# Narrow attention blocks finished four at a time, and a new order for all engines, in an attention and two-layer feed-forward kernel

## The chip, the cores and the metric

The kernel runs on one core of one Trainium2 chip. The metric is device time in microseconds (us), from the start of the program to its end; lower is better. Five kinds of instruction streams matter: TensorE (PE), VectorE (DVE), ScalarE (ACT), GpSimd (POOL), and SyncE (SP), whose single queue issues every DMA of this program.

## What is computed

The weights are float64, all else float32; q, k, v have 4 batches of 8 heads of 576 rows of 64. Attention keeps only the scores within tau of the row's maximum; its output, 2304 rows of 512, goes through two feed-forward layers with 2048 hidden units.

```python
scores = scale * np.matmul(q, k.transpose(0, 1, 3, 2))
thresh = np.max(scores, axis=-1, keepdims=True) - tau
scores = np.where(scores >= thresh, scores, -1000000000.0)
scores = scores - np.max(scores, axis=-1, keepdims=True)
attn = np.exp(scores)
attn = attn / (np.sum(attn, axis=-1, keepdims=True) + 1e-09)
return np.matmul(attn, v)
...
x = np.ascontiguousarray(attn_out.transpose(0, 2, 1, 3)).reshape(B * S, H * D)
h = x @ w_in
g = np.where(pos, h, np.where(neg, 0.0, (h + beta) ** 2 / (4.0 * beta)))
x = (g @ w_out).astype(np.float32)
...
h = x @ w_in
g = h - np.tanh(h)
return (g @ w_out).astype(np.float32)
```

## The kernel before

**Attention** works on blocks of 128 query rows of one head (`units`). A block goes through scores (`u_qk`, line 570, into one of three PSUM pairs `s0` to `s2`), row maximum (`u_max`, DVE), exponential and threshold (`u_exp`, ACT), masking with the row sum as a by-product (`u_mask`, line 603, DVE), a split of the weights into two float16 parts (`u_hi` on ACT, `u_lo` on POOL), and one DMA transposition (`u_tr`). There are five phases. Phase 0 is batch 0's 512 main rows of each head, phase 1 is batch 1; both are "narrow" (`NARROW = (0, 1)`). There the product with v is `u_dot` (line 658): 14 small matmuls of 64 columns into a bank of the two-bank ring `ph`, block by block, and `u_put` (line 677) brings the 128x64 result to SBUF (tile `xw`) while it multiplies by the reciprocal of the row sum. The reciprocal costs two one-column DVE instructions per block in `u_mask`. In the last head pair of phase 0 (`DIRECT = (3,)`) the weights are turned by TensorE instead of by DMA (`u_turn`, into `s2`), and `u_dot` is five float32 matmuls with the raw v (`vr`). Phases 2 to 4 are "wide" and use `pv` (line 743) in place of `u_dot` and `u_put`. `x_split` (line 771) turns a head pair's output with TensorE (`ph<-idt,xw`) and splits it into `xh` and `xl`.

**The feed-forward part** is 160 steps `j = (T, M, s)`: five token tiles T (512 columns, the last 256), two layers M, sixteen slices s of the hidden units. A step is `m_h` (12 matmuls into a `ph` bank), `m_act`, `m_dve`, `m_split`, and `m_out` (12 matmuls into `s1`, `s2`). During T = 0 the weights are loaded as 64-bit numbers (`w64`), decoded on ACT and DVE (`w_dec`, tiles `top` and `wr`), split (`w_split`) and stored to device memory (`w_store`, `wf`); later tiles load the stored parts (`w_get`).

**The order** is planned while the program is built. `agenda` (line 964) gives every operation a due time in steps: blocks of phase 0 lie before step 0, phase 1 is spread over the 32 steps of T = 0, phases 2 and 3 over T = 1 and T = 2. `PRE` (line 88) moves the due time of each kind of operation forward by so many steps, with one column for the time before step 0, one for T = 0, one for T = 1 to 3 and one for T = 4. `Program.issue` (line 261) then lays out all five streams: whichever engine is free first takes, of the operations whose inputs are there by the planner's own durations, the one that is due first. Those durations are written in `dve`, `act`, `sub`, `mm`, `dma`, and `Program.run`. What comes out is a fixed order per engine; on the chip each engine works through its list and waits where an input is late.

```python
    for i in range(NU):
        k = when(i)
        for fn, o in zip((u_qk, u_max, u_exp, u_mask, u_hi, u_lo, u_tr), UNIT):
            at(k + o, fn, i)
        if not units[i][0].wide:
            k = snap(k + lag(units[i][0]))
            at(k, u_dot, i)
            at(k, u_put, i)
```

Of the kernel before, what the change touches and what calls it, by code (L numbers as in the profile page):

```python
# [21 lines left out]
D = 64  # L22
# [63 lines left out]
    "A",  # L86
]
PRE = {
    "load_k": (7.27, -15.44, 8.94, 0.00),
    "load_q": (3.73, 6.44, 24.95, 0.00),  # L90
    "m_act": (0.00, -5.32, -0.24, -7.95),
    "m_dve": (0.00, 11.52, -21.89, -14.88),
    "m_evac": (0.00, -4.26, 4.07, -23.40),
    "m_h": (0.00, -1.15, -0.74, 2.14),
    "m_out": (0.00, -3.74, -0.36, 2.07),
    "m_split": (0.00, -1.26, 7.97, 1.61),
    "prep_k": (-15.59, 0.87, 7.96, 0.00),
    "prep_q": (21.35, 4.08, -22.11, 0.00),
    "pv": (0.00, 0.00, 2.86, 0.00),
    "u_dot": (-4.92, -3.40, 0.00, 0.00),  # L100
    "u_exp": (23.08, 16.66, 42.89, 0.00),
    "u_hi": (10.52, 34.89, 8.23, 0.00),
    "u_lo": (-15.45, 16.69, 11.25, 0.00),
    "u_mask": (1.51, -2.24, 3.82, 0.00),
    "u_max": (10.16, -1.25, -4.45, 0.00),
    "u_put": (19.81, -1.30, 0.00, 0.00),
    "u_qk": (-1.85, 25.10, 3.18, 0.00),
    "u_tr": (5.19, -3.00, 19.56, 0.00),
    "v_load": (1.71, -6.79, 1.05, 0.00),
    "v_max": (5.82, -0.49, -4.93, 0.00),  # L110
    "v_sc1": (-2.99, 15.36, 1.20, 0.00),
    "v_sc2": (-2.52, -2.20, 18.08, 0.00),
    "v_split": (9.81, -2.61, 10.15, 0.00),
    "w_dec": (3.79, -9.16, 0.00, 0.00),
    "w_get": (0.00, 21.91, 4.43, 25.50),
    "w_load": (-7.83, 28.33, 0.00, 0.00),
    "w_split": (5.66, -2.05, 0.00, 0.00),
    "w_store": (27.74, -13.05, 0.00, 0.00),
    "x_split": (17.49, 19.09, -2.78, 0.00),
    "x_tail": (0.00, 12.50, 0.00, 0.00),  # L120
}
G_LO = [
    "PPPVPPPV",
# [39 lines left out]
class Program:  # L163
# [65 lines left out]
    def run(self, o, t):  # L229

        e = o.eng
        if e == "SP":
            turn = o.dur > 1000
            begin = max(self.dma, t + (1000 if turn else 900))
            self.dma = begin + o.serve
            self.free[e] = max(t + o.dur, begin - (2000 if turn else 4500)) + 60
            return t, self.dma + 1250
        if e == "PE":
            load, f0, f1 = self.load, self.free[e], t - 250
            fill = 0  # L240
# [92 lines left out]
def attention_moe_moe2(ctx: ExitStack, tc: tile.TileContext, qd, kd, vd, tau, w1, w2, ident, out):  # L333
# [61 lines left out]
    def dve(name, **kw):  # L395
        src = kw.get("in_", kw.get("in0"))
        n = max(width(kw["out"]), width(src))
        ins = [kw[k] for k in ("in_", "in0", "in1") if k in kw]
        on_chip = not any(in_psum(a) for a in ins)
        fast = name in ("tensor_scalar", "tensor_copy") and on_chip and n > 8  # L400
        dur = 150
        if n > 8:
            dur = n / (1.92 if fast else 0.96) + 150 + 50 * ("accum_out" in kw)
            dur += 60 * (fast and any(isinstance(kw.get(k), AP) for k in ("scalar1", "scalar2")))
# [75 lines left out]
    for b, mains, tail in plan:  # L480
        for hp in range(H // 2):
            t = Obj()
            t.ph = len(touches) // 4
            t.direct = t.ph == 0 and hp in DIRECT
            t.b, t.hp, t.first, t.mains, t.tail = b, hp, len(units), mains, tail
            t.wide = t.ph not in NARROW
            t.aT = [None, None]
            t.cols = [slice(0, HALF), slice(HALF, S)] if mains and tail else [slice(0, 512) if mains else slice(512, S)]
            t.xf = t.xt = None
            touches.append(t)  # L490
            if tail:
# [166 lines left out]
    def u_dot(i):  # L658
        t, e, m = units[i]
        u = U[i]  # L660
        v = VQ[t.ph, t.hp // 2]
        u.p = ph_r()
        if t.direct:
            for c in range(5):
                n = 128 if c < 4 else 64
                mm(u.p[:, 0:D], u.et[0:n, 128 * c:128 * c + 128], v.raw[0:n, 2 * (t.hp % 2) + e, c], c == 0, c == 4)
            return
        for x in range(2) if e is None else (e,):
            h = 2 * (t.hp % 2) + x
            o = u.p[:, 64 * x:64 * x + 64] if e is None else u.p[:, 0:64]  # L670
            for c in range(5):
                mm(o, u.at[:, c], v.t[:, h, c, x, :], c == 0, False)
                mm(o, u.at[:, c], v.t[:, h, c, 1 - x, :], False, False)
            for c in range(4):
                mm(o, u.at[:, 5 + c], v.t[:, h, c, x, :], False, c == 3)

    def u_put(i):
        t, e, m = units[i]
        u = U.pop(i)
        if e is None:  # L680
            t.xt = xt_r()
        elif t.xf is None:
            t.xf = xf_r()
        for x in range(2) if e is None else (e,):
            o = t.xt[:, 64 * x:64 * x + 64] if e is None else t.xf[:, 128 * m + D * e:128 * m + D * e + D]
            src = u.p[:, 64 * x:64 * x + 64] if e is None else u.p[:, 0:64]
            if t.direct:
                dve("tensor_scalar", out=o, in0=src, scalar1=u.rs, scalar2=None, op0=ALU.mult)
            else:
                h = 2 * (t.hp % 2) + x  # L690
                dve("tensor_scalar", out=o, in0=src, scalar1=u.rs, scalar2=VQ[t.ph, t.hp // 2].inv[:, h:h + 1],
                    op0=ALU.mult, op1=ALU.mult)
# [412 lines left out]
```

## Time and profile before

| what | value |
|---|---|
| time, median of 3 runs | 1089.78 us (1081.36 to 1090.7) |
| span of the profiled execution, first to last instruction | 1082.6 us |
| PE busy | 1030.0 us (95%) |
| DVE busy | 629.2 us (58%) |
| ACT busy | 632.4 us (58%) |
| POOL busy | 504.0 us (47%) |
| DMA queue of the program | 271.83 MB, 86.5% of 16 engines' span |

The profile shows one execution. Of it the page gives the span, and no separate time for what lies around it; the span is 0.1% above the fastest of the three runs and 0.7% below their median. Busy shares are means over stages that differ much, so the rows below are read by stage. A matmul's record covers its passage through a pipeline, so a busy PE is not a PE at its peak. DMA share is the mean busy share of 16 engines and can be over 1, since an engine can have two transfers in hand. Nearly all instructions carry line 354, that of the recording helper; they are told apart by tile names.

### The profile page before, as it was taken

Reading aid. Unit: us, or ns where it says so; the run is one execution under the profiler, and the core shown is the slowest. Engines: PE = TensorE matmul, PEld = TensorE weight load, DVE = VectorE, ACT = ScalarE, POOL = GpSimd, SP = SyncE. Lnnn points to the kernel's source line nnn. Section 1 sums busy time; section 2 is a strip of 40 time slices with the busy share of each in tenths; the row PEclk is TensorE's granted clock in tenths of the full one; section 3 lists DMA queues with packets and bytes.
Section 4 is the critical chain, followed back from the end, with each engine's and each line's share of the span. In section 5 each row is a group of like instructions: output and inputs, shape, how many; then the busy total and the mean of one; then the engine's idle time right before and its main releaser. Section 6 shows DMA issues by size and latency. Waiting matters only on the chain.

```text
span 1082.6 us, 17257 instructions
## 1 busy us (share of the span) xinstructions
PE 1030.0 (95%) x5826; PEld 831.0 (77%) x5826; DVE 629.2 (58%) x1380; ACT 632.4 (58%) x1158; POOL 504.0 (47%) x510
## 2 busy tenths in 40 slices
PE   5789999999999999999999999999999999998997
PEld 3567777767777788778888888778877878888986
DVE  5987978898898766674347665742253331113432
ACT  5778777768776777676457777764353332222332
POOL 3654778768686555445345555444333212220000
PEclk8999999999999999999999999999999999999999
DMA  6999999999999998889679988897586655557997
GB/s 148 176 229 335 313 319 320 297 275 353 352 336 314 315 243 231 226 227 232 209 206 277 266 212 217 211 230 207 171 269 194 178 189 183 188 193 285 369 343 248
DMA packets 231384, 272.93 MB, mean 252 GB/s; under 512 B 170240, under 2 KB 170368, under 8 KB 231296
## 3 DMA queue, kind: packets, MB, share of 16 engines
q1 hardware_dynamic: 231296, 271.83, 86.5%
q8 instruction: 46, 0.75, 0.3%
q14 instruction: 42, 0.34, 0.1%
HBM read 193.40 MB, written 38.27 MB: 214 GB/s over the span
## 4 chain that ended last, share of the span: by engine, by line
PE 70%; DVE 12%; ACT 8%; DMA 5%; issue 4%; POOL 1%; SPq 0%; ACTq 0%; DVEq 0%; POOLq 0%
PE ph L354 35%; PE s L354 35%; DVE small L354 3%; DMA w<-in_w_dram 2%; ACT e L354 2%; DVE wr L354 2%; DVE e L354 2%; DMA vr<-in_vd_dram 2%; DVE g L354 1%; DVE xw L354 1%; ACT a L354 1%; DVE ph L354 1%; DMA wo<-wf0o 1%; ACT top L354 1%; DMA at<-w 1%
## 5 line engine op out<-in xcount | busy, mean ns | idle before, releaser
L354 PE MATMUL ph<-xh,wi 128*128 128x512 f32 x1024 | 271.1, 399 | 4.0 <-DVE g L354 3.7
L354 POOL TENSOR_TENSOR a<-e,a 128x512 f16<-128x512 f32 x236 | 180.9, 785 | 188.9 <-ACT a L354 172.4
L354 POOL TENSOR_TENSOR gl<-g,gh 128x512 fp32r<-128x512 f32 x114 | 152.3, 1336 | 199.1 <-ACT gh L354 179.4
L354 PEld LDWEIGHTS ph<-xh,wi 128*128 128x128 f32 x1024 | 188.0, 189 | 45.4 <-DVE g L354 6.2
L354 PE MATMUL s<-gh,wo 128*128 128x512 f32 (+1 forms) x640 | 157.4, 377 | 5.2 <-ACT gh L354 1.9
L354 PE MATMUL s<-wo,gh 128*128 128x512 f32 x576 | 155.1, 398 | 1.1 <-ACT w L354 0.7
L354 PE MATMUL ph<-xl,wi 128*128 128x512 f32 x512 | 144.8, 396 | 0.2 <-DVE xl L354 0.2
L354 DVE SCALAR_TENSOR_TENSOR e<-s,small,e 128x576 f32<-128x576 f32 x129 | 104.8, 813 | 67.1 <-ACT small L354 66.4
L354 DVE TENSOR_REDUCE small<-s 128x1 f32<-128x576 f32 x144 | 108.2, 752 | 47.7 <-PE s L354 46.8
L354 ACT ACTIVATE gh<-g 128x512 fp32r<-128x512 f32 (+1 forms) x152 | 88.2, 581 | 78.5 <-DVE g L354 76.2
L354 DVE TENSOR_TENSOR g<-ph,t 128x512 f32<-128x512 f32 (+1 forms) x80 | 50.8, 635 | 142.2 <-ACT t L354 138.9
L354 PEld LDWEIGHTS s<-gh,wo 128*128 128x128 f32 x640 | 112.0, 191 | 26.4 <-ACT gh L354 4.2
L354 PEld LDWEIGHTS s<-wo,gh 128*128 128x128 f32 x576 | 105.2, 188 | 22.9 <-ACT gh L354 1.1
L354 ACT ACTIVATE e<-s,small 128x576 f32<-128x576 f32 x129 | 94.9, 736 | 44.6 <-DVE small L354 41.7
L354 ACT ACTIVATE t<-ph 128x512 f32<-128x512 f32 (+1 forms) x80 | 44.1, 552 | 120.6 <-PE ph L354 120.4
L354 PEld LDWEIGHTS ph<-xl,wi 128*128 128x128 f32 x512 | 95.9, 188 | 23.2 <-DVE xl L354 1.2
L354 PE MATMUL s<-gl,wo 128*128 128x512 f32 (+1 forms) x320 | 89.4, 381 | 4.5 <-ACT xh L354 2.1
L354 DVE TENSOR_TENSOR ph<-ph,t 128x512 f32<-128x512 f32 (+1 forms) x80 | 51.4, 643 | 70.1 <-ACT t L354 69.2
L354 ACT ACTIVATE t<-ph,small 128x512 f32<-128x512 f32 (+1 forms) x80 | 51.4, 642 | 66.4 <-PE ph L354 66.2
L354 ACT ACTIVATE a<-e 128x576 f16<-128x576 f32 x118 | 80.1, 679 | 6.8 <-DVE e L354 4.8
L354 PE MATMUL s<-wo,gl 128*128 128x512 f32 x288 | 82.3, 393 | 1.0 <-ACT w L354 1.0
L354 PEld LDWEIGHTS s<-gl,wo 128*128 128x128 f32 x320 | 57.6, 190 | 15.8 <-ACT xh L354 3.4
(107 smaller groups left out, 1513.6 us busy)
## 6 DMA issues: line engine op xcount, KB each, us to landing
w<-in_w_dram SPq DMA_DIRECT2D x64, 512.0 KB, 6.0
wi<-wf0i SPq DMA_DIRECT2D x64, 512.0 KB, 4.1
wo<-wf0o SPq DMA_DIRECT2D x64, 512.0 KB, 4.3
wi<-wf1i SPq DMA_DIRECT2D x64, 512.0 KB, 3.8
wo<-wf1o SPq DMA_DIRECT2D x64, 512.0 KB, 3.7
kr<-in_kd_dram SPq DMA_DIRECT2D x32, 288.0 KB, 4.4
wf0i<-wi SPq DMA_DIRECT2D x16, 512.0 KB, 6.1
wf0o<-wo SPq DMA_DIRECT2D x16, 512.0 KB, 5.6
```

The costliest lines, as they stand in the source:

```text
L354: P.add(eng, dur, lambda: fn(**kw), outs, ins, serve, lock, load)
```

## The change

In the narrow phases the four blocks of a head become a group. `u_mask` writes the row sums of the four blocks side by side and makes no reciprocal; `g_rs` makes one pair of four-column instructions per head; `g_dot` does the matmuls of all four blocks into one `ph` bank, one after the other; `g_put` moves 128x4x64 results with one `tensor_tensor` and the reciprocals broadcast over 64 columns. All three are due when the head's fourth block would have been. The 64-row tail blocks keep the old form. Over the whole program DVE loses 64 reciprocals, 64 one-column `tensor_scalar` and 64 `xw<-ph` of 64 columns, and gains 16 of each in the four-fold form; PE, ACT, POOL and SP have the same instructions as before. The planner's numbers change as well: a plain DMA now counts as later and slower (345 in place of 415 bytes per ns), a transposition as 1200 in place of 1100, an issue on SP as longer; and all of `PRE` is replaced, of which two lines stand here.

```diff
@@ PRE
-    "m_split": (0.00, -1.26, 7.97, 1.61),
+    "g_rs": (78.75, 171.00, 0.00, 0.00),
+    "m_split": (0.00, -1.81, 25.05, -140.59),
...
-            begin = max(self.dma, t + (1000 if turn else 900))
+            begin = max(self.dma, t + (1050 if turn else 1250))
...
-        rec("SP", 590 if n < 200e3 else 345, nc.sync.dma_start, serve=max(n / 415.0, 130) + 150 * (n < 400e3), out=out, in_=in_)
+        rec("SP", 683 if n < 200e3 else 438, nc.sync.dma_start, serve=max(n / 345.0, 130) + 150 * (n < 400e3), out=out, in_=in_)
...
     def u_mask(i):
+        grouped = e is not None and not t.wide
+        if grouped:
+            if m == 0:
+                t.groups[e].sum = gs_r()
+            u.sum = t.groups[e].sum[:, m:m + 1]
...
+        if grouped:
+            return
         dve("tensor_scalar", out=u.sum, in0=u.sum, scalar1=1e-9, scalar2=1.0 / ASC if units[i][0].wide else 1.0, op0=ALU.add,
             op1=ALU.mult)
         dve("reciprocal", out=u.rs, in_=u.sum)
...
+    def g_rs(g):
...
+        scale = 1.0 if t.direct else VQ[t.ph, t.hp // 2].sc[:, h:h + 1]
+        dve("tensor_scalar", out=g.sum, in0=g.sum, scalar1=1e-9, scalar2=scale, op0=ALU.add, op1=ALU.mult)
+        dve("reciprocal", out=g.rs, in_=g.sum)
+
+    def g_dot(g):
...
+        g.p = ph_r()
+        for m in range(4):
+            u = U.pop(g.first + m)
+            o = g.p[:, 64 * m:64 * m + 64]
...
+    def g_put(g):
...
+        dve("tensor_tensor", out=t.xf.rearrange("p (m c) -> p m c", m=4)[:, :, D * e:D * e + D],
+            in0=g.p[:, 0:256].rearrange("p (m c) -> p m c", m=4),
+            in1=g.rs.rearrange("p (m o) -> p m o", o=1).to_broadcast([128, 4, D]), op=ALU.mult)
...
-            at(k, u_dot, i)
-            at(k, u_put, i)
+            if e is None:
+                at(k, u_dot, i)
+                at(k, u_put, i)
+            elif m == 3:
+                at(k, g_rs, t.groups[e])
+                at(k, g_dot, t.groups[e])
+                at(k, g_put, t.groups[e])
```

DVE before step 0, where the first two heads' results leave PSUM. Before (`small` holds sums and reciprocals, `e` and `wr` are weights being masked, `s0` to `s2` score banks):

```order
TENSOR_SCALAR xw_135<-ph1_139,small_64 128x64
TENSOR_REDUCE small_64<-s0_140 128x1
TENSOR_SCALAR xw_135<-ph0_138,small_64 128x64
RECIPROCAL small_64<-small_64 128x1 x2
SCALAR_TENSOR_TENSOR e0_123,small_64<-s2_142,small_64,e0_123 128x576
TENSOR_SCALAR xw_135<-ph1_139,small_64 128x64
TENSOR_REDUCE small_64<-s1_141 128x1
TENSOR_SCALAR xw_135<-ph0_138,small_64 128x64
RECIPROCAL small_64<-small_64 128x1
```

The same place now:

```order
TENSOR_TENSOR xw_135<-ph0_138,small_64 128x4x64
SCALAR_TENSOR_TENSOR wr_96,small_64<-s2_142,small_64,wr_96 128x576
SCALAR_TENSOR_TENSOR wr_96,small_64<-s0_140,small_64,wr_96 128x576
TENSOR_SCALAR small_64<-small_64 128x4
SCALAR_TENSOR_TENSOR wr_96,small_64<-s1_141,small_64,wr_96 128x576
RECIPROCAL small_64<-small_64 128x4
TENSOR_REDUCE small_64<-s2_142 128x1
TENSOR_TENSOR xw_135<-ph1_139,small_64 128x4x64
```

In the old rows four instructions each put one block's 64 columns away, between maxima, masks and reciprocals; in the new ones a single instruction does it for a whole head.

POOL before step 0, where batch 1's queries are prepared. Each pair of 512 and 64 columns is one block's low part, without which its transposition can't start (`w64` serves as space for it); `qtl0` and `qs0` are batch 1's queries, which nothing before step 0 reads. Before:

```order
TENSOR_TENSOR w64_97<-wr_96,w64_97 128x512
TENSOR_TENSOR qtl0_65<-qr0_120,qtl0_65 64x2x64
TENSOR_TENSOR qs0_121<-qr0_120,qs0_121 64x1024
TENSOR_TENSOR w64_97<-wr_96,w64_97 128x64
TENSOR_TENSOR w64_97<-wr_96,w64_97 128x512
```

Now:

```order
TENSOR_TENSOR a2_128<-wr_96,a2_128 128x512
TENSOR_TENSOR a2_128<-wr_96,a2_128 128x64
TENSOR_TENSOR w64_97<-wr_96,w64_97 128x512
TENSOR_TENSOR w64_97<-wr_96,w64_97 128x64
TENSOR_TENSOR qtl0_65<-qr0_120,qtl0_65 64x2x64
TENSOR_TENSOR qs0_121<-qr0_120,qs0_121 64x1024
```

The two query instructions stood inside the seventh block's pair and now stand behind the thirteenth block's. Likewise on SP the first load of v (`vr0`) was the seventh transfer behind that of tau and is now the fifth: the first half of `kr1` and the identity matrix no longer go ahead of it.

PE at the end of phase 0, up to the first matmul of step 0 (`ph0<-xh00,wi0`). `e2` is the last block of the last head, turned into `s2`; `vr0,at` are the direct products. Before:

```order
MATMUL ph0_138<-vr0_132,at1_130 128x64 x5
MATMUL ph1_139<-vr0_132,at1_130 128x64 x5
MATMUL s2_142<-idt_63,e2_125 128x128 x2
MATMUL ph1_139<-idt_63,xw_135 128x128 x3
MATMUL s2_142<-idt_63,e2_125 128x128 x2
MATMUL s2_142<-idt_63,e2_125 64x128
MATMUL ph0_138<-vr0_132,at1_130 128x64 x5
MATMUL s0_140<-kh1_115,qtl0_65 128x288 x2
MATMUL ph1_139<-idt_63,xw_135 128x128
MATMUL ph0_138<-xh00_76,wi0_98 128x512 x2
```

Now:

```order
MATMUL ph0_138<-vr0_132,at1_130 128x64 x4
MATMUL s2_142<-idt_63,e2_125 128x128 x4
MATMUL s2_142<-idt_63,e2_125 64x128
MATMUL ph0_138<-vr0_132,at1_130 128x64 x15
MATMUL s0_140<-kh1_115,qtl0_65 128x288 x2
MATMUL ph0_138<-vr0_132,at1_130 128x64
MATMUL ph1_139<-idt_63,xw_135 128x128 x4
MATMUL ph0_138<-xh00_76,wi0_98 128x512 x2
```

Behind the last turned block stood 5 direct products and one output transposition; now 16 and 4 stand there. In T = 0 to T = 3 the same steps stand in the same sequence, but the blocks of the wide phases come a little later: when the 47th of the 160 steps begins, PE has been given 320 score matmuls, in place of 336; a block is four of them. From step 113 on PE's order differs in a few places only, and SP's last 75 rows are the same.

## Rows read from the trace of the kernel before

**Rows 1.** The page's first line.
```profile
span 1082.6 us, 17257 instructions
```

**Rows 2.** Busy time by stage: length, PE, PEld, DVE, ACT, POOL, PEclk, DMA share, GB/s.
```profile
15.00:31.00 16.00, 12.04 (x60) 7.63 (x61) 14.71 (x45) 14.74 (x30) 9.81 (x13) 0.84 0.63 127
31.00:71.00 40.00, 30.93 (x342) 21.68 (x342) 37.36 (x121) 29.51 (x58) 28.36 (x38) 0.96 1.08 202
71.00:101.00 30.00, 28.86 (x203) 24.58 (x204) 22.07 (x58) 21.93 (x46) 10.87 (x10) 0.89 0.90 282
101.00:228.00 127.00, 119.15 (x767) 94.50 (x766) 104.77 (x220) 94.31 (x169) 95.98 (x84) 0.96 1.09 322
228.00:339.00 111.00, 106.64 (x723) 83.30 (x722) 97.49 (x184) 83.55 (x154) 85.23 (x74) 1.00 1.04 331
339.00:390.00 51.00, 49.39 (x240) 39.48 (x239) 37.75 (x86) 37.99 (x68) 27.39 (x31) 1.00 1.07 288
...
569.00:789.00 220.00, 217.63 (x1064) 175.17 (x1063) 120.50 (x266) 140.28 (x250) 107.80 (x115) 1.00 0.83 225
```

**Rows 3.** The same view in slices of 27 us, two of them.
```profile
216.00:243.00 27.00, 24.44 (x169) 18.49 (x168) 25.01 (x52) 18.52 (x37) 19.03 (x16) 1.00 0.90 272
...
297.00:324.00 27.00, 26.93 (x184) 21.47 (x184) 24.57 (x42) 21.55 (x40) 22.68 (x20) 1.00 1.12 347
```

**Rows 4.** Groups of DVE instructions from 0 to 101 us, two of the three kinds removed.
```profile
L354 DVE TENSOR_SCALAR xw<-ph,small 128x64 f32<-128x64 f32 x32 | 10.2, 320 | 2.7 <-PE ph L354 2.7
...
L354 DVE RECIPROCAL small<-small 128x1 f32<-128x1 f32 x32 | 4.8, 153 | 0.1
```

**Rows 5.** DVE in order of time: start us, us, instruction, idle before.
```profile
12.08 1.49 DVE L354 TENSOR_REDUCE small<-vr 128x4 f32<-128x1280 f32 x1 [3.65 <-DMA vr<-in_vd_dram]
...
48.75 0.68 DVE L354 TENSOR_TENSOR xl<-ph,xh 128x512 fp32r<-128x512 f32 x1
49.35 0.75 DVE L354 TENSOR_REDUCE small<-s 128x1 f32<-128x576 f32 x1
...
53.91 0.33 DVE L354 TENSOR_SCALAR xw<-ph,small 128x64 f32<-128x64 f32 x1
54.16 0.15 DVE L354 RECIPROCAL small<-small 128x1 f32<-128x1 f32 x1
54.23 0.14 DVE L354 TENSOR_SCALAR small<-small 128x1 f32<-128x1 f32 x1
54.28 0.81 DVE L354 SCALAR_TENSOR_TENSOR e<-s,small,e 128x576 f32<-128x576 f32 x1
```

**Rows 6.** SP's issues in order of time.
```profile
36.22 5.66 SPq L354 DMA_TRANSPOSE at<-w  x3
41.98 5.67 SPq L354 DMA_TRANSPOSE at<-a  x3
47.74 0.57 SPq L354 DMA_DIRECT2D kr<-in_kd_dram  x1
```

**Rows 7.** POOL in order of time.
```profile
31.35 0.55 POOL L354 TENSOR_TENSOR qtl<-qr,qtl 64x128 fp32r<-64x128 f32 x1
31.86 2.36 POOL L354 TENSOR_TENSOR qs<-qr,qs 64x1024 fp32r<-64x1024 f32 x1
```

**Rows 8.** PE in order of time, last direct products (two records per matmul), first step.
```profile
98.40 1.47 PE L354 MATMUL ph<-vr,at 128*128 128x64 f32 x10 [0.69 <-ACT at L354]
...
100.33 0.71 PE L354 MATMUL ph<-xh,wi 128*128 128x512 f32 x2
```

**Rows 9.** What PE waited for from 101 to 339 us: us in total, times, longest.
```profile
PE ph L354 <- DVE g L354: 3.8, 3, 2.0
PE s L354 <- DVE e L354: 2.9, 4, 2.0
...
PE ph L354 <- DMA at<-a: 0.4, 1, 0.4
```

**Rows 10.** DMA issues, transpositions: count, median us from issue to landing.
```profile
at<-a SPq DMA_TRANSPOSE x133, 4.4
```

More of the change, by code (lines that the diff above doesn't have):

```diff
@@ L88 @@
 PRE = {
[L89 to L95, printed above, removed]
-    "m_split": (0.00, -1.26, 7.97, 1.61),
[L97 to L120, printed above, removed]
+    "g_dot": (-0.91, -3.89, 0.00, 0.00),
+    "g_put": (9.30, 18.56, 0.00, 0.00),
+    "g_rs": (78.75, 171.00, 0.00, 0.00),
+    "load_k": (10.13, -15.18, 12.56, 0.00),
@@ new lines @@
+    "load_q": (10.80, 72.70, 81.88, 0.00),
+    "m_act": (0.00, -11.24, -42.70, -83.73),
+    "m_dve": (0.00, 43.72, 13.85, -112.10),
+    "m_evac": (0.00, 92.38, -36.86, -98.00),
+    "m_h": (0.00, 9.84, 0.58, 2.17),
+    "m_out": (0.00, -4.85, 0.56, 2.44),
+    "m_split": (0.00, -1.81, 25.05, -140.59),
+    "prep_k": (-82.50, 1.97, -102.20, 0.00),
+    "prep_q": (23.24, 33.59, -34.84, 0.00),
+    "pv": (0.00, 0.00, 191.38, 0.00),
+    "u_dot": (-4.92, -4.00, 0.00, 0.00),
+    "u_exp": (108.36, 89.20, 44.60, 0.00),
@@ new lines @@
+    "u_hi": (4.51, 121.56, -38.69, 0.00),
+    "u_lo": (25.51, 3.26, 37.17, 0.00),
+    "u_mask": (-1.37, -3.29, 45.50, 0.00),
+    "u_max": (31.05, 4.94, -49.80, 0.00),
+    "u_put": (19.81, 4.19, 0.00, 0.00),
+    "u_qk": (3.24, 68.45, 1.43, 0.00),
+    "u_tr": (1.97, -1.25, 104.61, 0.00),
+    "v_load": (10.43, 47.27, 96.99, 0.00),
+    "v_max": (-20.07, 31.57, -32.36, 0.00),
+    "v_sc1": (-8.56, 77.41, 1.72, 0.00),
+    "v_sc2": (34.40, -4.93, -1.52, 0.00),
+    "v_split": (31.70, 18.56, -14.07, 0.00),
@@ L121 @@
+    "w_dec": (6.34, -8.02, 0.00, 0.00),
+    "w_get": (0.00, 111.48, 49.96, 41.35),
+    "w_load": (-15.17, 0.13, 0.00, 0.00),
+    "w_split": (-3.55, -3.34, 0.00, 0.00),
+    "w_store": (-1.51, -14.46, 0.00, 0.00),
+    "x_split": (65.38, 54.28, -2.88, 0.00),
+    "x_tail": (0.00, 50.07, 0.00, 0.00),
 }
@@ L403, in dve @@
             dur = n / (1.92 if fast else 0.96) + 150 + 50 * ("accum_out" in kw)
-            dur += 60 * (fast and any(isinstance(kw.get(k), AP) for k in ("scalar1", "scalar2")))
+            scalars = sum(isinstance(kw.get(k), AP) for k in ("scalar", "scalar1", "scalar2"))
+            dur += 60 * (scalars > 0 and "accum_out" not in kw) + 55 * (scalars > 1)
         rec("DVE", dur, getattr(nc.vector, name), lock=n > 8 and on_chip and (fast or len(ins) == 2), **kw)
@@ L425, in dma @@
             n *= d
-        rec("SP", 590 if n < 200e3 else 345, nc.sync.dma_start, serve=max(n / 415.0, 130) + 150 * (n < 400e3), out=out, in_=in_)
+        rec("SP", 683 if n < 200e3 else 438, nc.sync.dma_start, serve=max(n / 345.0, 130) + 150 * (n < 400e3), out=out, in_=in_)
     idt = const("idt", [128, 128])
-    small = const("small", [128, 64])
+    small = const("small", [128, 80])
     tau_t, taun, tneg, qsc, half, none = (small[:, i:i + 1] for i in range(6))
@@ L471, in attention_moe_moe2 @@
     )
+    gs_r = Ring(lambda i: small[:, 52 + 4 * i:56 + 4 * i], 3)
+    gr_r = Ring(lambda i: small[:, 64 + 4 * i:68 + 4 * i], 3)
     m4_r = ring("m4", 2, [4, 1])
@@ L493, in attention_moe_moe2 @@
             t.done = [len(units) - 1] * 2
+            t.groups = []
             for e in range(2 if mains else 0):
+                if not t.wide:
+                    t.groups.append(Obj())
+                    t.groups[e].t, t.groups[e].e, t.groups[e].first = t, e, len(units)
                 for m in range(4):
@@ L567, in transpose @@
     def transpose(out, in_):
-        rec("SP", 1290, nc.sync.dma_start_transpose, serve=1100 * in_.shape[0] * width(in_) / (128 * 1152), out=out, in_=in_)
+        rec("SP", 1290, nc.sync.dma_start_transpose, serve=1200 * in_.shape[0] * width(in_) / (128 * 1152), out=out, in_=in_)
     def u_qk(i):
@@ L603, in u_mask @@
     def u_mask(i):
+        t, e, m = units[i]
         u = U[i]
-        u.sum = sum_r()
-        u.rs = rs_r()
+        grouped = e is not None and not t.wide
[3 more added lines that the diff above has]
+            u.sum = t.groups[e].sum[:, m:m + 1]
+        else:
+            u.sum = sum_r()
+            u.rs = rs_r()
         dve("scalar_tensor_tensor", out=u.e, in0=u.s, scalar=u.thr, in1=u.e, op0=ALU.is_ge, op1=ALU.mult, accum_out=u.sum
         )
+        if grouped:
+            return
         dve("tensor_scalar", out=u.sum, in0=u.sum, scalar1=1e-9, scalar2=1.0 / ASC if units[i][0].wide else 1.0, op0=ALU.add,
@@ L662, in u_dot, with dot @@
         u.p = ph_r()
[L663 to L668, printed above, removed]
-            h = 2 * (t.hp % 2) + x
[L670 to L675, printed above, removed]
+        for x in range(2):
+            h = 2 * (t.hp % 2) + x
+            o = u.p[:, 64 * x:64 * x + 64]
+            dot(o, u.at, v, h, x)
+    def dot(o, at, v, h, x):
+        for c in range(5):
+            mm(o, at[:, c], v.t[:, h, c, x, :], c == 0, False)
+            mm(o, at[:, c], v.t[:, h, c, 1 - x, :], False, False)
+        for c in range(4):
+            mm(o, at[:, 5 + c], v.t[:, h, c, x, :], False, c == 3)
     def u_put(i):
@@ L679, in u_put @@
         u = U.pop(i)
-        if e is None:
-            t.xt = xt_r()
-        elif t.xf is None:
-            t.xf = xf_r()
[L684 to L692, printed above, removed]
+        t.xt = xt_r()
+        for x in range(2):
+            o = t.xt[:, 64 * x:64 * x + 64]
+            h = 2 * (t.hp % 2) + x
+            dve("tensor_scalar", out=o, in0=u.p[:, 64 * x:64 * x + 64], scalar1=u.rs,
+                scalar2=VQ[t.ph, t.hp // 2].inv[:, h:h + 1], op0=ALU.mult, op1=ALU.mult)
+    def g_rs(g):
+        t = g.t
+        g.rs = gr_r()
+        h = 2 * (t.hp % 2) + g.e
+        scale = 1.0 if t.direct else VQ[t.ph, t.hp // 2].sc[:, h:h + 1]
+        dve("tensor_scalar", out=g.sum, in0=g.sum, scalar1=1e-9, scalar2=scale, op0=ALU.add, op1=ALU.mult)
+        dve("reciprocal", out=g.rs, in_=g.sum)
+    def g_dot(g):
+        t, e = g.t, g.e
+        v = VQ[t.ph, t.hp // 2]
+        h = 2 * (t.hp % 2) + e
+        g.p = ph_r()
+        for m in range(4):
+            u = U.pop(g.first + m)
+            o = g.p[:, 64 * m:64 * m + 64]
+            if t.direct:
+                for c in range(5):
+                    n = 128 if c < 4 else 64
+                    mm(o, u.et[0:n, 128 * c:128 * c + 128], v.raw[0:n, h, c], c == 0, c == 4)
+            else:
+                dot(o, u.at, v, h, e)
+    def g_put(g):
+        t, e = g.t, g.e
+        if t.xf is None:
+            t.xf = xf_r()
+        dve("tensor_tensor", out=t.xf.rearrange("p (m c) -> p m c", m=4)[:, :, D * e:D * e + D],
+            in0=g.p[:, 0:256].rearrange("p (m c) -> p m c", m=4),
+            in1=g.rs.rearrange("p (m o) -> p m o", o=1).to_broadcast([128, 4, D]), op=ALU.mult)
     VQ = {}
@@ L975, in attention_moe_moe2 @@
             at(k + o, fn, i)
-        if not units[i][0].wide:
-            k = snap(k + lag(units[i][0]))
-            at(k, u_dot, i)
-            at(k, u_put, i)
+        t, e, m = units[i]
+        if not t.wide:
+            k = snap(k + lag(t))
+            if e is None:
[5 more added lines that the diff above has]
+                at(k, g_put, t.groups[e])
     for t in touches:
```

## The prediction

> **What bounds the kernel now.** I read the page's span first, then busy time by stage, then in each stage who waits for whom. The span is 1082.6 us [rows 1]. The stages differ. From 15 to 101 us, phase 0 of the attention runs and no step of the feed-forward part has begun. From 31 to 71 us of it DVE is busy 37.36 of 40 us and PE 30.93; the DMA share is 1.08 [rows 2], and the highest share that a slice of T = 0 shows is 1.12 [rows 3]. So two things are nearly full there, DVE and the DMA engines. From 71 to 101 us it is PE that is full, 28.86 of 30 us; DVE has 8 us to spare [rows 2]. From 101 to 339 us (T = 0) PE is busy 225.8 of 238 us, and DVE 202.3; the DMA share is 1.09 and then 1.04 [rows 2]: near full again, but for a slice at 0.90 [rows 3]. From 569 to 789 us PE is busy 217.63 of 220 us and waits for next to nothing [rows 2]. A DVE saving can therefore pay before 71 us, partly in T = 0, and hardly after. That is where the narrow phases lie.
>
> **What goes from DVE.** Busy times overlap at their ends, so I price by the distance from one start to the next. Around 54 us: 53.91 to 54.16 is 0.25 us for one block's `xw`, 0.07 for its reciprocal, 0.05 for its `tensor_scalar` [rows 5]. That is 0.37 us a block, 1.48 a head. The new head has one reciprocal and one `tensor_scalar` of four columns, which I take at the same 0.12, and one `tensor_tensor` of 256 columns from PSUM. No row shows that one. Its bounds are 0.25 us (64 columns from PSUM) and 0.60 (512 columns from PSUM, 48.75 to 49.35) [rows 5]; by length it lies at 0.25 + 0.35 x 192/448 = 0.40. So a head costs 0.52 and saves 0.96 us (0.76 to 1.11). The 32 reciprocals and the 32 `xw` of phase 0 lie before 101 us [rows 4]; 24 blocks of these, six heads, are not turned by PE and come first: 5.8 us. All 16 heads give 15.4 us.
>
> **Before 71 us.** Three edits meet. The load of v goes out two transfers earlier; SP takes 0.57 us for such an issue [rows 6], and DVE stood 3.65 us at 12.08 for this load [rows 5]: 1.2 us earlier. The two query instructions on POOL, 0.55 + 2.36 = 2.9 us [rows 7], no longer delay the seventh block's low part; at that time DMA has room, with a share of 0.63 up to 31 us [rows 2], so blocks that come earlier can be turned earlier: between 0 and 2.9, I take 2. And DVE loses up to 5.8 us, but between 31 and 71 us the DMA share leaves only (1.12 - 1.08)/1.12 = 3.6% of 40 us, 1.4 us, if transpositions set the pace; I take 2.5, nearer to this end because SP shows six transpositions in a row at 1.9 us each [rows 6]. Sum: -5.7, say -6, between 0 and -9.9.
>
> *A rule that speaks against it.* SP issued three transpositions in 5.66 us and the next three in 5.67, with no wait between [rows 6]. The Trainium skill, Perfetto Trace Analysis, section "What 'DMA-bound' means", says that a stage can be bound by the sequencer that issues its DMAs, shown by a track filled with issue slices. For this stretch the trace looks like that. By that rule alone DVE's 5.8 us before 71 us would buy nothing; the result is the first rival below, whose time comes from the rows.
>
> **From 71 to 101 us.** The last head pair is turned by PE. Its dots now wait for the head's fourth block: behind the last turned block stand 16 float32 dots in place of 5. Five took 1.47 us [rows 8], so 16 take 4.7: 3.2 us more after the last arrival, less the 0.69 that PE stood there [rows 8]. But PE's work is the same in sum, so what stands later no longer stands earlier, and PE is the full engine here. DVE's two heads, 1.9 us, are covered by its idle 8 us. I take 0, between -1.9 and +3.2.
>
> *A second rule against it.* In the row at 98.40 the five dots wait only for their own block. The same page of the Trainium skill, section "Optimizing Scalar/DVE Operations", says that where such engines aren't saturated but cause bubbles elsewhere, breaking instructions up may let work finish sooner; this change does the reverse. By that rule the stage would cost the upper end, 3.2 us, and the sum below would be -7.3; that is the slow part of the forecast's own range, its four tenths within 1%.
>
> **T = 0.** Eight heads save 7.7 us of DVE. PE's waits for things that DVE made are 3.8 for `g` and 2.9 for `e` [rows 9], 6.7 us, the rest small. The DMA engines allow (1.12 - 1.09)/1.12 x 127 + (1.12 - 1.04)/1.12 x 111 = 3.4 + 7.9 = 11.3 us. A saving spread over 238 us hits a wait only where DVE is the last: I take -3, between 0 and -6.7. One `ph` bank is held for 56 dots in place of 14, but eight times in place of 32; I cost it at nothing, since PE waited 0.4 us in all for a turned tile there [rows 9], so the blocks come early and the steps' own work covers the rest; if that cover goes, it is the third rival.
>
> **After T = 0.** Four wide blocks stand later when the 47th step begins. Each brings a transposition of about 1.9 us of SP and DMA [rows 6], 7.6 us in a stretch that begins with a share of 1.07 (339 to 390 us) [rows 2]. PE pays for the blocks later, where it has 2.4 us of 220 free [rows 2]. I take -1.5, between -7.6 and +3.3 (16 score matmuls at that stage's mean of 217.63/1064 = 0.20 us). From step 113 on nothing that counts is moved: 0. The planner's new DMA numbers have no price of their own; what they do shows in the places above.
>
> **The sum:** -6 + 0 - 3 - 1.5 = -10.5 us. The profiled span goes from 1082.6 to 1072.1, by the factor 0.9903. The span lies 0.7% below the median of the three runs, so I carry the factor over: 1089.78 x 0.9903 = 1079.2, **1079 us**. A measurement of this kernel can tell about 1% from no change, 11 us; the forecast is just at that line.
>
> **Rivals.**
> 1. *DMA sets the pace.* Transpositions fill SP and the 16 engines before 71 us and the weights fill them in T = 0; DVE's saving turns into DVE idle time. For it: the shares of 1.08 and 1.09 [rows 2], the filled SP [rows 6]. Against it: 0.63 up to 31 us, and the slice at 0.90. What is left is the earlier v, 1.2 us, and 1.4 of slack: -3, 1079.2 + 7.5 = **1087 us**.
> 2. *Everything lands.* All 9.9 us before 71 us, 6.7 in T = 0, 6 of the 7.6 after it: -22.6, factor 0.979, **1067 us**. For it: DVE is busy 37.36 of 40 us from 31 to 71 us [rows 2], and DVE makes what PE waits for most in T = 0 [rows 9]. Against it: DMA shares leave room for less.
> 3. *A head's block of dots stands in PE's way.* In T = 0 the 56 dots of a head are one piece of PE's fixed order. If the fourth block's transposition is late on the chip, all behind it waits: the next step's `m_h`, then ACT, DVE, and the weights behind them. A transposition lands 4.4 us after its issue [rows 10]. If each of eight heads in T = 0 costs 2.8 us, between none and one landing, that is 22 us: 1079 + 22 = **1101 us**, slower. It decides from 1.3 us a head, where the forecast's gain is gone. Against it: the 0.4 us that PE waited for a turned tile in T = 0 [rows 9], and the order puts the dots where the planner, with slower DMA than before, has them ready.
>
> **How the numbers follow.** Forecast 0.45, with its own range 1071 to 1086; six tenths of it are faster by over 1%. DMA sets the pace: 0.22, within 1%. Everything lands: 0.21, faster. Dots in the way: 0.12, slower. So faster by over 1%: 0.27 + 0.21 = 0.48; within 1%: 0.18 + 0.22 = 0.40; slower by over 1%: 0.12. The range 1063 to 1091 holds the first three and leaves out the third rival and a little at the lower end.
>
> **What would show it.** Right: the first `ph<-xh,wi` of step 0 near 95 us, where it began at 100.33 [rows 8]; 16 `xw<-ph` of four times 64 columns starting the next instruction about 0.40 us later; fewer PE waits for `g` and `e` in T = 0; T = 0 three us shorter. The first rival: DVE idle before 71 us for `s` or `ph`, step 0 at 98. The third: PE waits for DMA `at` or for ACT behind the blocks of 56, above 10 us in sum. The forecast is wrong if step 0 starts no earlier than before, or if the stage from 569 us on grows by more than 4 us.

## The result, and the profile after

| kernel | median of its runs | range |
|---|---|---|
| before | 1088.31 us (4 runs) | 1081.36 to 1090.7 |
| changed | 1073.34 us (4 runs) | 1068.9 to 1075.22 |

The ratio is 0.9868, with a 95% interval of 0.9829 to 0.9906: 1.3% faster. The forecast was 1079 us with a range of 1063 to 1091. The profiled span fell from 1082.6 us [rows 1] to 1067.1. The page of the changed kernel begins so:

```profile
span 1067.1 us, 17085 instructions
...
PE 1023.6 (96%) x5826; PEld 827.4 (78%) x5826; DVE 609.3 (57%) x1236; ACT 633.5 (59%) x1158; POOL 502.3 (47%) x510
```

DVE's work fell by 19.9 us (629.2 before), more than the 15.4 that the prediction took from the heads; part of that is the new order's (runs 9 to 11). Busy time of the changed kernel in the stretches of [rows 2] (length, PE, PEld, DVE, ACT, POOL, PEclk, DMA share, GB/s):

```profile
15.00:31.00 16.00, 13.52 (x113) 8.72 (x114) 16.00 (x42) 15.50 (x36) 12.18 (x18) 1.00 1.08 195
31.00:71.00 40.00, 31.24 (x357) 24.12 (x353) 33.73 (x77) 30.05 (x59) 26.68 (x33) 0.91 1.13 222
71.00:101.00 30.00, 26.98 (x165) 22.30 (x163) 21.80 (x41) 25.45 (x50) 15.32 (x13) 0.97 0.91 319
101.00:228.00 127.00, 121.48 (x820) 98.52 (x819) 111.93 (x199) 97.23 (x178) 101.06 (x87) 0.98 1.09 314
228.00:339.00 111.00, 106.47 (x692) 84.90 (x691) 80.90 (x131) 75.45 (x133) 73.36 (x65) 0.98 1.08 337
```

From 15 to 31 us DVE is now full (14.71 of 16 before) and the DMA share is 1.08 in place of 0.63: blocks come early, and are turned early. From 31 to 71 us DVE has 6.3 us to spare.

The first score block turned by PE (`s<-idt,e`) and the first matmul of step 0, PE in order of time, before:

```profile
70.90 0.84 PE L354 MATMUL s<-idt,e 128*128 128x128 f32 x5 [1.56 <-DVE e L354]
...
100.33 0.71 PE L354 MATMUL ph<-xh,wi 128*128 128x512 f32 x2
```

and after:

```profile
60.42 0.77 PE L357 MATMUL s<-idt,e 128*128 128x128 f32 x5 [3.00 <-DVE e L357]
...
90.27 0.72 PE L357 MATMUL ph<-xh,wi 128*128 128x512 f32 x2
```

Step 0 begins 10.1 us earlier, and nearly all of that is there by the first turned block, 10.5 us.

**A trap in reading the later stages.** By the first matmul of each tile, T = 0 became 1.6 us longer and T = 1 7.7 us shorter. But PE's order changed at those borders: 23 of T = 0's `m_out` matmuls that stood behind the first matmul of T = 1 now stand ahead of it, and some score matmuls went the other way. In the trace two starts lie 0.23 us apart for the first kind and 0.13 for the second, so the work that changed sides can be taken out:

| stretch | before, us | after, us | difference | work that changed sides | at equal PE work |
|---|---|---|---|---|---|
| to step 0 | 100.3 | 90.3 | -10.1 | none | -10.1 |
| T = 0 | 238.8 | 240.4 | +1.6 | +23 `m_out`, -4 scores: +4.8 | -3.2 |
| T = 1 | 229.6 | 221.9 | -7.7 | -23 `m_out`, -12 scores: -6.9 | -0.8 |
| T = 2 and 3 | 401.2 | 403.3 | +2.0 | +16 scores: +2.1 | -0.1 |
| T = 4 to the end | 112.6 | 111.3 | -1.3 | none | -1.3 |

What PE waited for in T = 0 of the changed kernel, the answer to [rows 9] (us, times, longest):

```profile
PE ph L357 <- DVE xw L357: 3.2, 3, 2.1
PE s L357 <- DVE e L357: 2.1, 3, 1.2
PE s L357 <- ACT gh L357: 2.1, 1, 2.1
PE ph L357 <- DVE g L357: 1.4, 1, 1.4
```

`g` and `e` fell from 6.7 to 3.5 us; the wait for `xw` grew from 1.1 to 3.2, which fits a head's result that comes in one piece; run 10 below shows whose the fall is.

### The profile page after: what moved, and what is told of

It reads as the page before. It is cut to its first block, busy times and chain, and to the rows that moved or that the text cites. A ratio compares the mean times of both kernels' runs of the same rounds, so it can differ in the third digit from the quotient of the medians.

```text
span 1067.1 us, 17085 instructions
## 1 busy us (share of the span) xinstructions
PE 1023.6 (96%) x5826; PEld 827.4 (78%) x5826; DVE 609.3 (57%) x1236; ACT 633.5 (59%) x1158; POOL 502.3 (47%) x510
## 4 chain that ended last, share of the span: by engine, by line
PE 81%; DVE 6%; DMA 4%; ACT 4%; issue 2%; POOL 2%; SPq 1%; ACTq 0%; DVEq 0%; POOLq 0%
PE s L357 41%; PE ph L357 40%; DVE small L357 2%; DMA vr<-in_vd_dram 1%; DVE e L357 1%; DMA w<-in_w_dram 1%; DVE wr L357 1%; SPq L357 1%; ACT e L357 1%; DVE g L357 1%; DMA wf0i<-wi 0%; DVE xw L357 0%; DMA qr<-in_qd_dram 0%; POOL a L357 0%; ACT xh L357 0%
## 5 line engine op out<-in xcount | busy, mean ns | idle before, releaser
L357 POOL TENSOR_TENSOR gl<-g,gh 128x512 fp32r<-128x512 f32 x114 | 154.7, 1357 | 231.1 <-ACT gh L357 207.0
L357 ACT ACTIVATE gh<-g 128x512 fp32r<-128x512 f32 (+1 forms) x152 | 88.3, 582 | 72.4 <-DVE g L357 70.9
L357 PEld LDWEIGHTS ph<-xl,wi 128*128 128x128 f32 x512 | 95.7, 188 | 24.9 <-DVE xl L357 2.5
L357 ACT ACTIVATE e<-e,small 128x576 f32<-128x576 f32 x76 | 58.9, 775 | 33.9 <-DVE small L357 33.6
```

The costliest lines, as they stand in the source:

```text
L357: P.add(eng, dur, lambda: fn(**kw), outs, ins, serve, lock, load)
```

## The experiments

Theory A: DVE's saving and the new order each carry a part, and DMA paces T = 0. Rivals: the grouping alone carries the gain (G), or the order alone (O). "Before" is timed anew beside each set: 1086.4, 1088.3 and 1088.0 us.

**1. Grouping with the old numbers of the planner.**

```diff
 PRE = old table, with
+    "g_dot": old u_dot, "g_put": old u_put, "g_rs": old u_put
 old DMA and DVE costs in the planner
```

> Grouping alone: the four-block form with all of the planner's old numbers (old table, old DMA costs). Theory A (order and saving each carry a part; DMA paces T = 0): of DVE's 5.8 us before step 0 about half lands, step 0 near 97 us (94 to 100) where before has 100.3 and the change 90.3; T = 0 stays at 239 +-3; T = 1 stays near 229.6, since the wide blocks stay early; total near 1085. Rival G (the grouping carries the whole gain): step 0 near 91, T = 1 near 222, total near 1073. Rival O (the order carries it): step 0 at 100, total 1088.

Measured: 1084.23 us, ratio 0.997 (0.9936 to 1.0003); step 0 at 95.5, T = 0 243.5, T = 1 230.8. Its waits in T = 0:

```profile
PE s L357 <- DVE e L357: 4.9, 8, 1.9
PE ph L357 <- ACT wi L357: 4.7, 2, 3.3
PE ph L357 <- DVE g L357: 3.1, 3, 1.7
```

G falls. Theory A's total and step 0 are met, its T = 0 (239 +-3) is not: the head start of 4.8 us at step 0 is lost again in T = 0, where PE stands for split weights (`wi`) that it didn't wait for before.

**2. The new numbers without the grouping.**

```diff
 kernel before, with the new PRE (without g_*) and the new costs in the planner
```

> The new table and the new planner costs, blocks put away one by one as before. Theory A: step 0 near 94 us (91 to 97), T = 0 239 +-3, T = 1 near 222, total near 1079. Rival G (grouping carries it): step 0 near 100, T = 1 229, total near 1088. Rival O (order carries it): step 0 near 90, total near 1073.

Measured: 1087.68 us, ratio 1.0019 (0.9995 to 1.0043); step 0 at 96.6, T = 0 245.8, T = 1 227.6. Its waits in T = 0:

```profile
PE s L354 <- DVE e L354: 7.9, 9, 2.3
PE ph L354 <- DVE g L354: 4.9, 4, 1.8
```

O falls in this form, and theory A's total of 1079 is missed as well: the same numbers, given other instructions, plan another order, and that one makes PE wait 12.8 us for `e` and `g`. Neither half brings 5 us alone; both together bring 15 to 18.

**3. Only the wide phases' numbers.**

```diff
 kernel before, with the third and fourth column of PRE from the change
```

> The kernel before with only the third and fourth column of the table (T = 1 to 4) from the change; the order is word for word that of before until about step 24. Theory A (wide blocks start later, out of the full DMA stretch at the start of T = 1): step 0 at 100.3 and T = 0 near 239 as before, T = 1 near 222 instead of 229.6, T = 2 near 222 instead of 220; total 5 to 6 us below before, near 1082.5. Rival (T = 1 gained because of how T = 0 ended): T = 1 stays near 229.6, total as before.

Measured: 1087.82 us, ratio 1.001 (0.9987 to 1.0033); step 0 at 98.0, T = 0 238.2, T = 1 234.8, T = 2 222.0. The expectation for T = 1 and the total was wrong: T = 1 didn't shrink, although its blocks come later. From 336 us on PE waits for a stored weight and for `g`:

```profile
PE ph L354 <- DMA wi<-wf0i: 2.1, 1, 2.1
PE ph L354 <- DVE g L354: 2.0, 1, 2.0
```

I had read T = 1's 7.7 us as a gain by later blocks. It was this miss that sent me to the table above, where 6.9 of them are work that changed sides.

**4. Half of the weight stores left out, order unchanged.**

```diff
-                dma(wf[M][p][s], W[j].flat[p])
+                dma(...) for even s alone; w_get reads slice s - s % 2
```

> The changed kernel, order of all engines the same, but the split weights of the odd slices aren't stored, and T = 1 to 4 load the even slice's in their place (so the output of later tiles is from other weights). Half of 33.5 MB of stores goes out of T = 0. Theory A (DMA paces T = 0): T = 0 falls from 240.4 to about 229, PE's busy time there, or a little above (229 to 233). Rival (T = 0 is paced by PE's waits for what DVE and ACT make, or by the blocks of 56 dots): T = 0 stays within 238 to 241. Step 0 at 90.3 by both.

Measured: 1071.24 us; T = 0 240.4, the same as in the change:

```profile
92.70:333.10 240.40, 229.06 (x1510) 184.61 (x1509) 195.92 (x330) 176.02 (x315) 180.77 (x155) 0.98 0.96 259
```

The DMA share is 0.96 in place of 1.08, and T = 0 is not shorter. PE is busy 229.06 us there, and its four longest waits are for `xw`, `gh`, `e` and `g`, as in the change. DMA doesn't pace T = 0; that part of theory A falls.

**5 and 6. DVE's old work at the new order.** The planner lays out the grouped form; what is issued at the same places are the single instructions. Phase 0 alone, then phase 1 alone.

```diff
-        dve("reciprocal", out=g.rs, in_=g.sum)
+        for m in range(4): tensor_scalar and reciprocal of column m
...
-        dve("tensor_tensor", out=t.xf... 128x4x64, in1=g.rs broadcast)
+        for m in range(4): tensor_scalar(out=xf 64 columns, in0=g.p 64 columns, scalar1=g.rs[:, m])
```

> The changed kernel, every engine's order the same, but in phase 0 each head's three four-fold DVE instructions are issued as four pairs of one column and four transfers of 64 columns at the same place: about 1.0 us more DVE per head (3 x 0.12 + 4 x 0.25 - 0.33), 6 us for the six heads that come first. Theory A (DVE bounds the stretch before step 0, so its saving lands there): step 0 at 94 to 97 us where the same order began at 90.3 and 92.7 in two runs; total 1077 to 1080. Rival O (what counts is the new order, DVE's saving buys nothing by itself): step 0 at 90 to 93, total 1073.

Measured: 1075.71 us, ratio 0.9894 (0.9831 to 0.9957). Against 60.42 and 90.27:

```profile
66.80 1.33 PE L358 MATMUL s<-idt,e 128*128 128x128 f32 x5 [3.23 <-DVE e L358]
...
97.80 0.71 PE L358 MATMUL ph<-xh,wi 128*128 128x512 f32 x2
```

> The same for phase 1 alone: 8 us more DVE spread over the 240 us of T = 0, all orders as in the change. Theory A (PE's waits in T = 0 are for what DVE makes): step 0 at 90 to 93 as in the change, and at equal PE work the end of T = 0 comes 3 to 5 us later; total 1076 to 1079. Rival (T = 0 gained by the order): end of T = 0 and total within 1 us of the change, 1073.

Measured: 1074.52 us, ratio 0.9897 (0.9861 to 0.9933); step 0 at 92.5, T = 0 243.7. In both the stage grows as A says (step 0 of run 5 by a little more than its 94 to 97), but both totals lie below A's (1077 to 1080, 1076 to 1079). They stand 2.4 and 1.2 us above the change's first four runs; four to six runs can't tell 2 us.

What is put back isn't quite the old work. In the kernel before, a reciprocal and a `tensor_scalar` that stand side by side belong to different blocks, and the two take 0.12 us from start to start [rows 5]. Here every reciprocal stands right behind the `tensor_scalar` whose result it reads, and the two take 0.30:

```profile
27.57 0.19 DVE L744 TENSOR_SCALAR small<-small 128x1 f32<-128x1 f32 x1
27.79 0.16 DVE L746 RECIPROCAL small<-small 128x1 f32<-128x1 f32 x1
27.87 0.20 DVE L744 TENSOR_SCALAR small<-small 128x1 f32<-128x1 f32 x1
```

The `xw<-ph` of 64 columns are a little shorter than before, 0.28 us long in place of 0.33. So runs 5, 6 and 10 bound the worth of DVE's saving from above; by how much is said under runs 9 to 11.

**7 and 8. Two single moves taken back.** The query preparation among the first seven blocks again; the load of v behind `kr1`.

```diff
+ ACT: qtl0, qs0, qr0 behind the second, fourth and seventh block's u_hi; POOL: qtl0, qs0 inside the seventh block's pair
```
```diff
+ SP: vr0 behind the second half of kr1
```

> The changed kernel with batch 1's first query preparation (three instructions on ACT, two on POOL) back at its old places among blocks 1 to 7, nothing else moved. Theory A: the seventh block's low part comes 2.9 us later and all blocks behind it: step 0 2 to 3 us later, 92.5 to 95.5; total 1075 to 1076. Rival (POOL has room there): step 0 at 90 to 93, total 1073.

> The changed kernel with the first load of v one place behind both halves of kr1, as near to its old place as it gets without moving anything else. Theory A: DVE's first maximum over v begins 0.8 to 2 us later than 8.95 (before-like orders showed 9.8 to 12.1), and step 0 by as much, 91 to 95; total 1074 to 1075. Rival (the wait is absorbed before DVE becomes the bound): step 0 unmoved at 90 to 93, total 1073.

Measured: 1072.87 and 1073.01 us. With the queries back, the maximum over v began at 10.13 and step 0 at 95.7; run 6, where it began at 10.22, had step 0 at 92.5: 3.3 us for the queries. With v late:

```profile
11.22 1.49 DVE L379 TENSOR_REDUCE small<-vr 128x4 f32<-128x1280 f32 x1 [2.81 <-DMA vr<-in_vd_dram]
```

and step 0 at 96.9. The profiles show both prices, the totals neither; since step 0 of one and the same order lies between 90.3 and 92.7, I leave their size open.

**9 to 11. The change again, both phases apart, and before again, on one chip.**

> The changed kernel once more, as the measure for the three beside it and for how far step 0 moves from run to run: all theories expect 1073 +-2 us, step 0 between 90 and 93, T = 0 at 240.4 +-0.5, T = 1 at 221.9.

> The changed kernel's order of every engine with the DVE work of before: the four-fold instructions issued as four single ones in phases 0 and 1, 16 us more DVE. Theory A (DVE's saving lands before step 0 and at PE's waits in T = 0): step 0 at 96 to 98, T = 0 at 243.7, total 7 to 10 us above the change run beside it, 1080 to 1083. Rival O (the order carries the gain): total within 2 us of the change.

> The kernel before once more, for the spread of its step 0: by the arrival of v in other runs with the old load order (9.8 to 12.1 us) step 0 between 97.5 and 101, T = 0 at 238.8 +-0.5, T = 1 at 229.6.

Measured: the change 1070.06 us, ratio 0.9835 (0.9806 to 0.9864); apart in both phases 1079.41, ratio 0.9917 (0.9887 to 0.9948); before 1088.01 over 11 runs, the profiled one 1090.37. Up to step 0 (columns as above), the change, apart, and before:

```profile
0.00:92.20 92.20, 72.74 (x612) 55.26 (x613) 70.96 (x158) 67.64 (x136) 52.07 (x71) 0.94 0.97 226
```
```profile
0.00:99.20 99.20, 74.21 (x612) 56.40 (x613) 79.81 (x230) 68.69 (x136) 51.95 (x71) 0.91 0.86 199
```
```profile
0.00:101.70 101.70, 76.07 (x613) 56.20 (x613) 77.66 (x231) 68.53 (x136) 52.33 (x71) 0.91 0.91 211
```

Some expectations are missed by a little: the change's total (1073 +-2) and T = 0 (238.6), step 0 of run 10 (99.2) and of run 11 (101.7), T = 0 of run 10 (241.5) and T = 1 of run 11 (231.3).

With single instructions DVE is busy 8.9 us more before step 0 than in the change, but the kernel before only 6.7 (77.66). Counted by how far each of them moves the end of DVE's work on, all `xw<-ph` and the reciprocals with their `tensor_scalar` take 29.9 us up to the end of T = 0 in the kernel before (run 11), 33.7 in run 10 and 20.2 in the change (run 9). So run 10 puts back 13.5 us where the grouping took away 9.7. At an unchanged order the work put back costs 1079.4 - 1070.1 = 9.3 us; DVE's saving is worth that at most, and about 7 in proportion (an estimate). The other 8.6 (1088.0 - 1079.4) to 11 are the order's. In the two profiles, whose spans are 9.5 us apart, 2.4 of the order's part are at step 0 (101.7 against 99.2) and, at equal PE work, about 2 each in T = 0, in T = 1, and in T = 2 and 3, and 1 at the end. That division rests on one pair: the two profiles of the kernel before, with one and the same order, are themselves 6 us apart (1082.6 and 1088.6). So DVE's saving is at most half of the gain, and run 1 shows little of it with the old numbers of the planner.

**12. The maximum over v taken out of the way.**

```diff
+ DVE: v_max behind the third mask, the scaling of kr1 behind the fourth; PE: v_sc1's transposition two blocks later
```

> The changed kernel with DVE's maximum over v behind the third mask, the scaling of kr1 behind the fourth and PE's transposition of the maxima two blocks later; nothing else moved. Theory A (DVE standing for v at 8.9 to 11.2 us sets back the whole chain of blocks): first mask at 9.2 instead of 11.0 us, no wait for v, step 0 1.5 to 4 us earlier than in the run beside it, 87 to 90; total 1.5 to 3 us below the change. Rival (the first blocks are paced by loads and transpositions behind): step 0 and total unmoved within 1 us.

Measured: 1070.18 us beside 1070.06; step 0 at 92.7. No wait for v is left, but DVE stands for PE's second score block all the same:

```profile
9.69 0.76 DVE L380 TENSOR_REDUCE small<-s 128x1 f32<-128x576 f32 x1 [1.16 <-PE s L380]
...
13.92 1.48 DVE L380 TENSOR_REDUCE small<-vr 128x4 f32<-128x1280 f32 x1
```

The first mask begins at 10.37 in place of the 9.2 expected, and the rival holds: the 1.5 us of the maximum itself, moved out of the way, gain nothing. In the run beside it (9) it began at 8.44 without a wait for v, so the pair says nothing on the price of such a wait. No run beats the change.

## Why the prediction was right, and which term was mis-sized

Step 0 and the first turned block in the profiles of three forms:

| order and DVE work | first turned block, us | step 0, us |
|---|---|---|
| before's order (before, 3, 11) | 70.9, 69.5, 71.7: mean 70.7 | 100.3, 98.0, 101.7: mean 100.0 |
| the change's (after, 4, 6, 9) | 60.4, 62.0, 62.6, 60.7: mean 61.4 | 90.3, 92.7, 92.5, 92.2: mean 91.9 |
| the change's, phase 0 apart (5, 10) | 66.8, 68.2: mean 67.5 | 97.8, 99.2: mean 98.5 |

- **Before 71 us, forecast -6 (0 to -9.9): measured -9.3 (-10.5 in the first pair).** This is the mis-sized term, and the failed step is "between 31 and 71 us the DMA share leaves only (1.12 - 1.08)/1.12 = 3.6% of 40 us", by which DVE's part was cut to 2.5. Up to the first turned block (columns as above; before, run 5, the change):

```profile
0.00:70.90 70.90, 48.69 (x412) 32.97 (x412) 56.69 (x174) 47.50 (x91) 41.40 (x62) 0.93 0.88 177
```
```profile
0.00:66.80 66.80, 46.36 (x343) 32.28 (x343) 56.73 (x166) 47.01 (x91) 41.31 (x63) 0.91 0.87 180
```
```profile
0.00:60.42 60.42, 42.60 (x343) 29.36 (x343) 50.89 (x118) 46.66 (x91) 41.56 (x63) 0.97 1.00 199
```

  With 5.8 us more of DVE work in front of it, at an unchanged order, the block comes 6.1 us later (61.4 to 67.5): one for one. A share of 1.12 was no ceiling: it went to 1.13, and between 15 and 31 us it rose from 0.63 to 1.08, room of which the step took no account for DVE. The row that decided was DVE's 37.36 of 40 us [rows 2]. That the 6.1 equals the 5.8 at which six heads were priced is chance, since run 5 puts back more than the old form took. In the kernel before DVE is as busy as in run 5 up to this mark, partly with other work that the new order does later, and stands idle about 3 us longer (by the means of the table): the other 3.2 us of the 9.3 are the order's. The v and query terms (-1.2 and -2) sum to as much, but the runs don't separate them from the rest of the order. The maximum over v began at 9.8 to 12.1 us in four profiles with the load at its old place, and at 8.4 to 10.2 in eight with the new one, means 10.8 and 9.4.
- **From 71 to 101 us, 0 (-1.9 to +3.2): +1.2**, from the first turned block to step 0 (30.5 against 29.3).
- **T = 0, -3 (0 to -6.7): -3.2 at equal PE work. The size is right, the reason isn't borne out.** The term was to come from PE's waits for `g` and `e`, and they did fall, from 6.7 to 3.5 us. But with phase 1 apart they stay as low, 3.7 us in run 6 and 3.8 in run 10, where other waits are longer than in the change (in run 10 1.1 for `kh` and 0.6 for `wi`, at most 0.4 for either in the change):

```profile
PE ph L358 <- DVE g L358: 1.9, 2, 1.4
PE s L358 <- DVE e L358: 1.9, 2, 1.2
PE s L358 <- ACT kh L358: 1.1, 1, 1.1
```

  So that fall is the new order's. With phase 1 apart T = 0 took 243.7 and 241.5 us (runs 6 and 10); seven profiles with phase 1 as in the change (after, 4, 5, 7, 8, 9, 12) lie at 238.6 to 242.2, mean 240.2. That is 2.4 us for the work put back, with a spread of the same size. The test named for it, "T = 0 three us shorter", was badly chosen: read between first matmuls, T = 0 grew.
- **After T = 0, -1.5 (-7.6 to +3.3): -2.2** in the first pair (-0.8 - 0.1 - 1.3). The size is right, the reason isn't shown: run 3 moves the wide blocks alone and gains nothing.
- **The price of a head.** The new `tensor_tensor` was put at 0.40 us between starts; it is 0.33 (30.81 to 31.14 below). The pair in front of it was put at 0.12, but the four-column `tensor_scalar` alone takes 0.5 on average before step 0 (last section), and a reciprocal about 0.1 behind it. So a head costs about 0.9, not 0.52, and saves about 0.6 in place of 0.96 (an estimate from these rows), below the range of 0.76 to 1.11. A price too high and a ceiling too low erred in opposite directions; that the range held owes something to this luck.
- **Rivals.** "DMA sets the pace" falls in both places: by run 4 in T = 0, by run 5 before 71 us, where 6 us of DVE work move the blocks by 6 us. With it falls that reading of SP's track: it was filled with issues [rows 6], and it didn't bind at that amount of DVE work. Whether it or the DMA engines bind in the changed kernel, where DVE has 6.3 of 40 us to spare and the share is 1.13, no run shows. In the changed kernel four transpositions in a row are issued at 1.43 us each, 1.9 in [rows 6], so the length of such a slice isn't a fixed cost of SP. The Trainium skill's Perfetto Trace Analysis, "What 'DMA-bound' means", takes a filled track of the issuing engine as a sign of that bound; the trace of the kernel before, beside run 5, doesn't bear it out.

```profile
23.57 5.71 SPq L357 DMA_TRANSPOSE at<-w  x4
```

"Everything lands" was right in size before 71 us (-9.3 of its -9.9, but not by its parts) and too high in T = 0. "Dots in PE's way" shows as the 2.1 us by which the wait for `xw` grew, not as 22.

## What to carry to other kernels

Price a saving by the engine that is full in its stretch, and use a busy share of DMA as a limit only after a run that takes DMA work away has moved the time. Where an order is planned anew, compare stages at equal work: the same mark in both programs can have other work in front of it. A planner's tuned numbers fit one set of instructions; to price the instructions alone, keep the order and change only what is issued in it, and measure what the work put back takes there (here 13.5 us for 9.7).

## What was not expected of the hardware

DVE of the changed kernel in order of time:

```profile
26.72 0.87 DVE L357 TENSOR_SCALAR small<-small 128x4 f32<-128x4 f32 x2
...
30.81 0.41 DVE L357 TENSOR_TENSOR xw<-ph,small 128x256 f32<-128x256 f32 x1
31.14 0.80 DVE L357 SCALAR_TENSOR_TENSOR wr<-s,small,wr 128x576 f32<-128x576 f32 x1
...
57.69 1.74 DVE L357 TENSOR_SCALAR small<-small 128x4 f32<-128x4 f32 x2
```

The four-column `TENSOR_SCALAR` of the new head, priced like a one-column one at 0.05 us between starts, takes up to 1.27 us: two of them hold DVE from 57.69 to 59.34. The one-column form in run 5 takes 0.13 to 0.21, and the four-column form that reads PSUM 0.12 to 0.13. POOL was at work at that time:

```profile
56.88 1.41 POOL L357 TENSOR_TENSOR kl<-kr,kh 128x576 fp32r<-128x576 f32 x1
58.24 1.42 POOL L357 TENSOR_TENSOR w<-wr,w 128x512 f16<-128x512 f32 x2
```

The Trainium skill, SBUF — State Buffer, section "Who interferes with whom", says that a `tensor_scalar` from SBUF to SBUF can go into a mode that uses the port pair shared with GpSimd, and that whoever comes second waits for the other's whole instruction. The rows agree with it: the two end at 58.31 and 59.42, each about 0.03 us behind the POOL instruction that was running (58.29 and 59.40); the second and its POOL instruction start 0.02 us apart, so which of them came first isn't shown. Of the sixteen up to the end of T = 0, eleven take 0.35 to 1.27 us, and each of these ends 0.02 to 0.03 us behind a POOL instruction that it overlaps; the other five take 0.16 to 0.22. The one-column form of run 10 takes 0.13 to 0.21 beside POOL instructions of over 1 us too. Up to step 0 the eight instructions kept DVE busy for 4.1 us, where eight at 0.14 would be 1.1:

```profile
L357 DVE TENSOR_SCALAR small<-small 128x4 f32<-128x4 f32 x8 | 4.1, 530 | 0.0
```

The mean clock that PE was granted up to step 0 (1.00 is 2.4 GHz throughout, a mean below it has time at 1.2 GHz in it) was 0.91, 0.93 and 0.91 in the profiles of before's order (before, 3, 11), 0.96, 0.93, 0.94 and 0.94 in those of the change's (after, 4, 6, 9), and 0.91 with DVE's old work (5 and 10). The same 612 or 613 matmuls kept PE busy for 76.9 us before and 71.3 after; how much of step 0's gain is the clock's own isn't separated.
